# An attention kernel ordered by a planner: other figures for its additions by DMA, a little more lead for the score products, other seeds and one more vector batch

## The chip, the cores and the metric

The kernel runs on one core of one Trainium2 chip. The time is device microseconds of one launch, the median of several runs; one more execution is taken by the hardware profiler, and every profile line here is from such an execution.

## What is computed

Two attention branches over the same 2048 tokens of width 512, with 32 heads of 16, mixed by a gate for each token:

```python
x = A_x
g = sigmoid((x * gate_w).sum(-1, keepdims=True))
# A: softmax attention
scores = einsum("bhqd,bhkd->bhqk", q, k) * 16 ** -0.5
o = einsum("bhqk,bhkd->bhqd", softmax(scores), v)
a = o.reshape(B, S, D) @ A_wo
# B: linear attention, phi(t) = [softmax(t @ w_phi), softmax(-t @ w_phi)]
kv, z = einsum("bhsf,bhsd->bhfd", phi_k, v), einsum("bhsf->bhf", phi_k)
o = einsum("bhqf,bhfd->bhqd", phi_q, kv) / (einsum("bhqf,bhf->bhq", phi_q, z) + 1e-6)
b = o @ B_wo
return g * a + (1 - g) * b
```

Inputs and output are bf16.

## The kernel before

**Tiles.** Branch A has 2048 tiles of scores, 128 keys by 512 queries of one head. Four of them (four heads, on four strips of 32 rows of TensorE) are a pack; 512 packs make 32 groups of 16, and a group's value products gather in one PSUM bank, its accumulator. Most tiles go to ScalarE: TensorE multiplies two (`_qk`, L1185) into a ring of four PSUM banks, ScalarE takes the exponential of both at once into the ring `ET` of 16 slots (`_exp`, L1233), and TensorE multiplies four slots by `V` (`_pv`, L1296). An exponential may write a slot only when the value product that reads it is done.

**Vector batches.** The other tiles go to VectorE in batches of four (`_vector_batch`). For each tile TensorE makes the scores in a bank outside the ring, and VectorE turns them into the bits of an approximate exponential: `v_bits` (L1043) scales and rounds to a 16-bit integer, one tile or two neighbouring banks at a time. The value is a mean over four shifted copies of these bits, so a batch needs three more tiles of integers: `v_step` on VectorE (L1072, four tiles at once), an addition on GpSimd (L1085), or an addition by DMA from the constant `steps` (L1077, 512 KB, issued by GpSimd). Which of them is used goes by the batch's kind. Each of the four copies is multiplied with `V` or `V2` into the group's accumulator (L1296 again, reading `va`, `vb` or the spare memory of `va_wt`, `va_vb`, `vb_on` and `WB`). `NUMS` says how many batches each of the 32 groups has.

**Around them.** Projections (L808, L816, L855, L923) are four products each and an evacuation on VectorE; branch B runs in between (L1457 to L1668, its exponential L1494 on ScalarE); every group ends with a transposition and a division (L1317 to L1349), every four groups with output products (L808 on `WoA` and `WoB`), copies (L1819 to L1829) and stores. Filler products (L1205, L1303) keep TensorE from falling idle.

**The order.** Nothing runs in the order in which it is written. `Plan` holds all operations with a cost, a priority and what they depend on; `order` walks through time, picks on each engine what can start first and, among those, what ranks first, and so writes five queues, one for each engine. Each engine then takes its queue strictly in order, waiting on semaphores. The planner's figures only set the order; on the chip every wait is real. Three of its rules matter here:

- An addition by DMA goes through one channel: it starts `FIRST` after its issue or when the channel is free, takes `MOVES`, and has landed `LANDED` later. What reads its tile is ordered for that time.
- `_late` refuses other work to TensorE if it would end too late for the next score product of ScalarE; `SLIP` moves that border.
- `shift` adds a pseudo-random amount to every priority, from a new entry of `SEEDS` after every 8 packs, so other seeds give another order from the first pack on.

Of the kernel before, what the change touches and what calls it, by code (L numbers as in the profile page):

```python
# [70 lines left out]
class Plan:  # L71
# [6 lines left out]
    SWITCH, PASS, STEP = 0.097, 0.2155, 0.004  # L78
    SPAN, SHARE, FILL = 3.0, 0.58, 0.2155
    PAD, PADS, OVER = 0.45, 2, 0.2  # L80
    SLIP, GAPS, FLOOR = -0.015, 0.65, 0.46

    def __init__(self):
        self.ops = []
# [58 lines left out]
        self.ops.append(o)  # L143
        return o

    SEEDS = (46439, 36297, 2531, 40950, 971, 19659, 43523, 55019, 18035, 35534, 32147, 43513, 5583, 38153, 15135, 20962, 59679, 30439, 26213, 19105, 29455, 34877, 55135, 21414, 3210, 43195, 29993, 1363, 20599, 10691, 26101, 32053, 19915, 10799, 30427, 37694, 56714, 13257, 35679, 20623, 23887, 52907, 36031, 9619, 51019, 11311, 52185, 0, 13385, 43491, 31707, 19759, 44590, 53230, 9789, 22249, 59009, 3577, 57594, 35439, 52351, 16746, 45215, 2875)
    EVERY = 8
    FIRST, LANDED, TURN, HOLD = 1.5, 1.5, 1.9, 30.0

    def shift(self):  # L150

        if len(self.SEEDS) <= self.drawn or self.now < self.EVERY * self.drawn:
            return
        s = self.SEEDS[self.drawn]
        self.drawn += 1
# [329 lines left out]
class _Kernel:  # L485
# [26 lines left out]
    LAST, FIRST_OUT, NEXT_OUT, DEP_OUT = 0, 3, 0, 2  # L512
    ALONE, EARLY = 12, 10
    C_MIX, C_POOL, SPREAD = 15.5, (0.2, 0.0011), 0.9
    C_ADD, MOVES, ADD_AT, PVD, U3 = 0.9, 2.9, -1, 0, 2
    L_MIX, L_BACK, L_PHIT, L_ONTB = 6.5, 0.4, 0.9, 0.4
    TWOS, BEGIN, SPLIT, PSPLIT = 2, 44, 262, 1
    PHIT2, ONTB2, C_PHIT2, C_ONTB2 = 1, 1, 2.3, 1.9
# [460 lines left out]
                prio=100))  # L979
        self.b_gB.writers = done  # L980

    NUMS = (1, 4, 5, 4, 4, 5, 4, 5, 4, 5, 4, 6, 5, 4, 4, 5, 5, 5, 5, 4, 4, 5, 4, 5, 4, 5, 5, 5, 6, 6, 5, 4)

    def _plan_vector(self):

        NT, away = self.NT, []
        for g in range(self.NPACK // NT):
            n = self.NUMS[g]
            rest = self.REND if g == self.NPACK // NT - 1 else self.REST
# [885 lines left out]
```

## Time and profile before

| | |
|---|---|
| median of 3 runs | 724.36 us (723.66 to 725.03) |
| the profiled execution | 723.53 us, of which the span from first to last instruction is 721.7 |
| TensorE / VectorE / ScalarE / GpSimd busy | 694.0 / 691.5 / 706.4 / 447.8 us |
| exponentials of two tiles (L1233, 128x1024) | 730, 674.9 us |
| `v_bits` of one tile / of two | 458 / 63 |
| additions by DMA (L1077) | 157 |
| TensorE's clock | 1.00 throughout |

A row of the page's groups names a line, the engine and the operation, what is written and read (buffer numbers left out), the count, the busy time, the mean of one, and the idle time just before with what ended it. "PE ps L1185" is TensorE, writing PSUM, at line 1185. PEld is TensorE's weight load, which runs beside its products. The chain of waits follows the last instruction back through what released it. Instructions of one engine overlap a little at their ends, so a duration is longer than the pitch at which they follow each other.

### The profile page before, as it was taken

The page shows a single profiled execution, that of the slowest core. Times are in us where ns is not written, and L with a number is a line of the kernel's source. Part 1 is how long each engine was busy: PE and PEld are TensorE (multiplying, and loading weights), DVE is VectorE, ACT ScalarE, POOL GpSimd, SP SyncE. Part 2 cuts the span into 40 slices and gives each one's busy share as a digit, 9 for nine tenths or more (in the row PEclk, how much of TensorE's full clock was granted, in tenths as well). Part 3 has the DMA queues.
Part 4 walks back from the last instruction along what each step waited for, and adds up shares of the span by engine and source line. Part 5 has one row for each costly group of instructions (what it writes and reads, how often), then busy time and mean ns, then how long its engine had stood idle before and what let it go on. Part 6 is the DMA issues. An engine that isn't in the chain of part 4 may idle for free.

```text
span 721.7 us, 17384 instructions
## 1 busy us (share of the span) xinstructions
PE 694.0 (96%) x7312; PEld 211.7 (29%) x7375; DVE 691.5 (96%) x1143; ACT 706.4 (98%) x756; POOL 447.8 (62%) x567
## 2 busy tenths in 40 slices
PE   8999999999999999999999999999999999999998
PEld 3332232222333222222222233232323232223222
DVE  4999999999999999999999999999999999999997
ACT  5999999999999999999999999999999999999996
POOL 3332566665675747485768775768758678477552
PEclk9999999999999999999999999999999999999999
DMA  9623676684966778966768877678678577868873
GB/s 226 155 50 74 123 136 119 116 158 94 189 117 118 147 143 169 187 121 118 140 122 157 166 146 146 105 147 159 114 135 163 112 155 147 151 129 150 165 139 88
DMA packets 68557, 99.17 MB, mean 137 GB/s; under 512 B 42752, under 2 KB 47872, under 8 KB 68480
## 3 DMA queue, kind: packets, MB, share of 16 engines
q0 software_dynamic: 22608, 82.32, 60.4%
q1 hardware_dynamic: 44000, 14.96, 10.3%
q8 instruction: 57, 0.93, 0.5%
q10 hardware_dynamic: 1872, 0.79, 0.5%
q14 instruction: 20, 0.16, 0.1%
HBM read 4.21 MB, written 2.10 MB: 9 GB/s over the span
## 4 chain that ended last, share of the span: by engine, by line
ACT 65%; PE 20%; DVE 7%; DMA 3%; POOL 2%; issue 1%; SPq 1%; POOLq 0%
ACT ET L1233 63%; PE ps L1185 7%; PE ps L1296 7%; PE ps L808 5%; ACT bq L1494 2%; DVE va L1043 2%; DVE vb L1072 1%; DMA va<-steps 1%; DMA vb<-steps 1%; SPq L673 1%; DMA xT<-in_A_x_dram 1%; DVE va_vb L1043 1%; POOL va L1077 0%; DVE onB L1668 0%; PE ps L923 0%
## 5 line engine op out<-in xcount | busy, mean ns | idle before, releaser
L1233 ACT ACTIVATE ET<-ps 128x1024 bf16<-128x1024 f32 (+1 forms) x734 | 677.1, 1084 | 3.1 <-PE ps L1185 1.6
L1043 DVE TENSOR_SCALAR va<-ps 128x512 uint16<-128x512 f32 (+1 forms) x438 | 312.6, 745 | 13.1 <-PE ps L1185 12.1
L1185 PE MATMUL ps<-qT,kT 32*128 32x512 bf16 (+1 forms) x2052 | 292.3, 384 | 13.3 <-ACT ET L1233 7.7
L1077 POOL DMA_DIRECT2D va<-steps x106 | 107.1, 1061 | 103.6 <-DVE vb L1072 50.2
L1185 PEld LDWEIGHTS ps<-qT,kT 32*128 32x128 bf16 x2052 | 74.0, 91 | 277.5 <-ACT ET L1233 255.8
L1296 PE MATMUL ps<-ET,V 128*32 128x512 bf16 x1464 | 141.9, 388 | 0.7 <-DVE va L1043 0.7
L1072 DVE TENSOR_SCALAR vb<-va 128x2048 uint16<-128x2048 uint16 x147 | 100.3, 695 | 0.2 <-PE ps L1296 0.2
L1296 PE MATMUL ps<-va,V 128*32 128x512 bf16 x984 | 92.3, 384 | 0.3 <-DVE vb L1072 0.3
L1296 PE MATMUL ps<-vb,V 128*32 128x512 bf16 x896 | 84.1, 384 | 0.6 <-DMA vb<-steps 0.3
L1085 POOL TENSOR_TENSOR vb<-vb,steps 128x512 int32<-128x512 int32 x50 | 64.0, 1299 | 26.7 <-DVE vb L1072 19.2
L1296 PEld LDWEIGHTS ps<-ET,V 128*32 128x32 bf16 x1464 | 36.4, 94 | 66.9 <-issue 59.0
L808 PE MATMUL ps<-WB,xT 128*128 128x512 bf16 x164 | 49.6, 383 | 3.6 <-issue 2.4
L1498 POOL TENSOR_TENSOR btree<-btree 128x512 f16<-128x512 f16 (+1 forms) x32 | 30.3, 947 | 22.2 <-DVE vb L1072 12.7
L1303 PE MATMUL ps<-kT,zero 128*32 128x512 bf16 x492 | 43.1, 383 | 0.0
L1077 POOL DMA_DIRECT2D vb<-steps x28 | 33.7, 1203 | 8.2 <-PE ps L808 3.7
L808 PE MATMUL ps<-xT,WA 128*128 128x512 bf16 x102 | 32.4, 384 | 2.0 <-issue 1.3
L1043 DVE TENSOR_SCALAR va_vb<-ps 128x512 uint16<-128x512 f32 (+1 forms) x47 | 33.7, 734 | 0.1
L1296 PEld LDWEIGHTS ps<-va,V 128*32 128x32 bf16 x984 | 24.3, 95 | 27.9 <-issue 20.8
L1494 ACT ACTIVATE bq<-bq 128x2048 bf16<-128x2048 bf16 x16 | 31.4, 1960 | 0.0
L899 POOL TENSOR_SCALAR qT<-qT,mask 128x512 bf16<-128x512 bf16 x30 | 22.8, 761 | 12.1 <-DVE qT L895 6.2
L1296 PEld LDWEIGHTS ps<-vb,V 128*32 128x32 bf16 x896 | 22.0, 95 | 24.3 <-issue 14.3
L1043 DVE TENSOR_SCALAR va_wt<-ps 128x512 uint16<-128x512 f32 (+1 forms) x36 | 25.9, 738 | 0.1
(123 smaller groups left out, 721.2 us busy)
## 6 DMA issues: line engine op xcount, KB each, us to landing
va<-steps POOLq DMA_DIRECT2D x106, 512.0 KB, 6.3
vb<-steps POOLq DMA_DIRECT2D x28, 512.0 KB, 7.0
va_wt<-steps POOLq DMA_DIRECT2D x10, 512.0 KB, 5.9
va_vb<-steps POOLq DMA_DIRECT2D x10, 512.0 KB, 5.5
WB<-in_B_wqkv_dram SPq DMA_DIRECT2D x1, 1536.0 KB, 8.2
vb_on<-steps POOLq DMA_DIRECT2D x3, 512.0 KB, 6.7
out_dram<-outt SPq DMA_DIRECT2D x12, 128.0 KB, 6.3
WA<-in_A_wqkv_dram SPq DMA_DIRECT2D x2, 384.0 KB, 4.4
```

The costliest lines, as they stand in the source:

```text
L808: return e.matmul(out, lhs, rhs, start=start, stop=stop)
L899: x = self.plan.op("POOL", lambda e, side=side: e.tensor_scalar(self.qT[:, s0 + side, :], raw, self.mask[:, side:side + 1], 0.0, op0=ALU.m ...
L1043: bits = lambda e, to, src: e.tensor_scalar(to, src, SCALE * LOG2E * 128.0, float(ORIGIN), op0=ALU.mult, op1=ALU.add)
L1072: o = op("DVE", lambda e: e.tensor_scalar(whole(dst), whole(va), float(by), None, op0=ALU.add), 0.16 + n * QCH * 0.00026, reads=reads, wri ...
L1077: o = self.dma("POOL", f"add{number}_{k}", lambda e: e.dma_start(tile[:, 0:n], self.steps[:, 0:n], accum_op=ALU.add), cost=self.C_ADD, rea ...
L1085: o = op("POOL", lambda e, lo=lo, hi=hi: e.tensor_tensor(whole(v3)[:, lo:hi].bitcast(I32), whole(v1)[:, lo:hi].bitcast(I32), whole(self.st ...
L1185: return e.matmul(out[:, cols], self.kT[32 * i:32 * i + 32, cp, kt * TOK:(kt + 1) * TOK], self.qT[32 * i:32 * i + 32, s, cols], start=True ...
L1233: o = plan.op("ACT", lambda e: e.activation(self.ET[:, a % NS:a % NS + n, cols], self.ps[:, a % NR:a % NR + n, cols], ACT.Exp, scale=SCALE ...
L1296: ins = e.matmul(self._bank(ot)[32 * i:32 * i + 32, :], v[:, v0:v0 + 32], tile, start=(kt == 0), stop=(kt == self.NT - 1), tile_position=( ...
L1303: ins = e.matmul(self._bank(ot)[32 * i:32 * i + 32, :], self.zero[:], self.kT[:, 0, 0:QCH], start=False, stop=False, tile_position=(0, 32 ...
L1494: op("ACT", lambda e: e.activation(flat, flat, ACT.Exp), 1.789, reads=[b], writes=[b], name="b_exp", prio=due + 1)
L1498: + [("b_sum", two(128 * n), lambda e, n=n: e.tensor_tensor(half[:, :, 0:n], half[:, :, 0:n], half[:, :, n:2 * n], ALU.add), (n <= self.P_ ...
```

## The change

Four constants and two tables differ; no operation of the kernel is written differently.

```diff
-    SLIP, GAPS, FLOOR = -0.015, 0.65, 0.46
+    SLIP, GAPS, FLOOR = -0.04, 0.65, 0.46
...
-    SEEDS = (46439, 36297, 2531, 40950, 971,
...
+    SEEDS = (20645, 24735, 11770, 21495, 24798,
...
-    FIRST, LANDED, TURN, HOLD = 1.5, 1.5, 1.9, 30.0
+    FIRST, LANDED, TURN, HOLD = 1.4, 1.2, 1.9, 30.0
...
-    C_ADD, MOVES, ADD_AT, PVD, U3 = 0.9, 2.9, -1, 0, 2
+    C_ADD, MOVES, ADD_AT, PVD, U3 = 0.9, 2.85, -1, 0, 2
...
-    NUMS = (1, 4, 5, 4, 4, 5, 4, 5, 4, 5, 4, 6, 5, 4, 4, 5, 5, 5, 5, 4, 4, 5, 4, 5, 4, 5, 5, 5, 6, 6, 5, 4)
+    NUMS = (2, 4, 5, 5, 4, 5, 4, 4, 5, 4, 5, 4, 5, 4, 5, 5, 4, 5, 4, 5, 4, 5, 4, 5, 5, 5, 5, 5, 5, 6, 6, 4)
```

All 64 seeds are others. `NUMS` adds up to 147 where it was 146, so four tiles of scores go from ScalarE to VectorE, and it spreads them otherwise: the first group has two batches for one. Since the seeds and the planner's figures reach every choice, nearly the whole of TensorE's, VectorE's and GpSimd's queues stands in another order. By number of instructions the built program has 728 exponentials of two tiles for 730, 466 `v_bits` of one tile for 458 and 61 of two for 63, 236 `v_step` for 235, 159 additions by DMA for 157, and 118 passes of filler products at L1303 for 123.

The prediction shows TensorE's order at two places, the first 19 us and the end. In its rows L1185 is a product of scores, L1296 a product of values (reading `ET` it is ScalarE's tile, reading `va`, `vb`, `WB` a vector batch's), L808 with `WA` a projection of queries or keys, with `WoA` and `WoB` the output, and L923 a projection of values.

At the start, TensorE before, from the last-but-one score row ahead of the first value product:

```order
L1185 MATMUL ps<-qT,kT 128x512 x3
L923 MATMUL ps<-WA,xT 128x2x128 x4
L1185 MATMUL ps<-qT,kT 128x512 x3
L1296 MATMUL ps<-ET,V 32x512 x8
L923 MATMUL ps<-WA,xT 128x2x128 x8
L808 MATMUL ps<-xT,WA 128x512
L1185 MATMUL ps<-qT,kT 128x512 x3
```

and in the change, from the score row that holds the same two tiles of ScalarE as the third row above:

```order
L1185 MATMUL ps<-qT,kT 128x512 x3
L808 MATMUL ps<-xT,WA 128x512
L923 MATMUL ps<-WA,xT 128x2x128 x8
L1296 MATMUL ps<-ET,V 32x512 x4
L923 MATMUL ps<-WA,xT 128x2x128 x4
L1296 MATMUL ps<-ET,V 32x512 x4
L1296 MATMUL ps<-va_96,V 32x512 x4
L1296 MATMUL ps<-ET,V 32x512 x4
L1185 MATMUL ps<-qT,kT 128x512 x4
```

A projection and eight products of values' projections moved from behind the first value product to ahead of it. At the end, TensorE's rows from the last scores on, before:

```order
L1185 MATMUL ps<-qT,kT 128x512 x2
L808 MATMUL ps<-WoA,onTA 128x512 x3
L808 MATMUL ps<-WoB,WT 128x512 x2
L1296 MATMUL ps<-ET,V 32x512 x4
L1296 MATMUL ps<-va_100,V_67 32x512 x4
L1296 MATMUL ps<-va_97,V_67 32x512 x4
L1296 MATMUL ps<-vb_104,V_67 32x512 x4
L808 MATMUL ps<-WoB,WT 128x512 x2
L808 MATMUL ps<-WoA,onTA 128x512 x6
L808 MATMUL ps<-WoB,WT 128x512 x4
L808 MATMUL ps<-WoA,onTA 128x512 x7
```

and in the change:

```order
L1185 MATMUL ps<-qT,kT 128x512 x2
L1296 MATMUL ps<-ET,V 32x512 x4
L1296 MATMUL ps<-va_96,V_67 32x512 x4
L1296 MATMUL ps<-ET,V 32x512 x4
L1296 MATMUL ps<-WB,V_67 32x512 x4
L1296 MATMUL ps<-ET,V 32x512 x8
L1296 MATMUL ps<-va_97,V_67 32x512 x4
L1296 MATMUL ps<-vb_101,V_67 32x512 x4
L1296 MATMUL ps<-va_98,V_67 32x512 x4
L808 MATMUL ps<-WoB,WT 128x512 x4
L808 MATMUL ps<-WoA,onTA 128x512 x13
```

Before, 5 output products stand between the last scores and the last exponential's value product, and 19 behind the last value product; in the change none and 17, so 7 moved ahead of the last scores.

More of the change, by code (lines that the diff above doesn't have):

```diff
@@ L144, in op @@
         return o
-    SEEDS = (46439, 36297, 2531, 40950, 971, 19659, 43523, 55019, 18035, 35534, 32147, 43513, 5583, 38153, 15135, 20962, 59679, 30439, 26213, 19105, 29455, 34877, 55135, 21414, 3210, 43195, 29993, 1363, 20599, 10691, 26101, 32053, 19915, 10799, 30427, 37694, 56714, 13257, 35679, 20623, 23887, 52907, 36031, 9619, 51019, 11311, 52185, 0, 13385, 43491, 31707, 19759, 44590, 53230, 9789, 22249, 59009, 3577, 57594, 35439, 52351, 16746, 45215, 2875)
+    SEEDS = (20645, 24735, 11770, 21495, 24798, 57639, 39767, 34826, 20859, 44155, 52338, 33183, 53515, 39123, 29127, 37122, 1099, 17207, 36203, 5703, 52058, 34843, 7471, 28503, 58027, 39163, 28279, 57222, 57234, 36322, 36955, 4803, 37407, 40227, 14797, 24150, 35511, 21954, 11343, 9845, 38167, 791, 56855, 27221, 49278, 20251, 58495, 48113, 23517, 41183, 44671, 35093, 13874, 3235, 32949, 53535, 26359, 52383, 21199, 31586, 32878, 1351, 27747, 20999)
     EVERY = 8
-    FIRST, LANDED, TURN, HOLD = 1.5, 1.5, 1.9, 30.0
+    FIRST, LANDED, TURN, HOLD = 1.4, 1.2, 1.9, 30.0
     def shift(self):
```

## The prediction, made before the result was known

> **What bounds the kernel now.** I read the page first: the span, the busy time of each engine, and the rows of 40 slices that say where an engine is not full.
>
> ```profile
> span 721.7 us, 17384 instructions
> PE 694.0 (96%) x7312; PEld 211.7 (29%) x7375; DVE 691.5 (96%) x1143; ACT 706.4 (98%) x756; POOL 447.8 (62%) x567
> DVE  4999999999999999999999999999999999999997
> ACT  5999999999999999999999999999999999999996
> ```
>
> ScalarE is the fullest, and it is short of full only in the first and the last slice. The next view, busy time by stretch, and the groups of ScalarE alone in the same stretch, say how short it is between them:
>
> ```profile
> 19.00:713.00 694.00, 672.22 (x7179) 202.86 (x7241) 677.80 (x1117) 693.56 (x740) 440.45 (x549) 1.00 0.71 136
> L1233 ACT ACTIVATE ET<-ps 128x1024 bf16<-128x1024 f32 x723 | 668.2, 1088 | 0.4
> 200.00:300.00 100.00, 96.88 (x1052) 28.62 (x1055) 99.56 (x166) 100.00 (x109) 65.18 (x81) 1.00 0.78 148
> 500.00:600.00 100.00, 95.73 (x1072) 28.84 (x1072) 98.87 (x163) 99.80 (x106) 71.46 (x91) 1.00 0.74 140
> ```
>
> The columns are the stretch, its length, then the busy time of PE, PEld, DVE, ACT and POOL, the clock, the DMA engines' share and GB/s. From 19 to 713 us ScalarE works 693.56 of 694.00 us: it has lost 0.44 us in the whole middle of the kernel. VectorE has 16.2 us idle there and TensorE 21.8, and from 200 to 300 us VectorE ran 99.56% full while ScalarE lost nothing. So the time is three pieces: the start until ScalarE runs without a gap, the sum of its exponentials, and the tail behind the last of them. What is taken from ScalarE shortens the kernel, provided nothing new makes it wait.
>
> **The change: work taken and given.** The prices are pitches in the chain of waits, where instructions follow without a gap; durations in the groups overlap their neighbours and would count too much.
>
> ```profile
> 147.83 35.78 ACT ET L1233 x39
> 108.16 1.13 DVE va L1043
> 110.09 0.60 DVE vb L1072
> 110.83 1.80 DVE va L1043 x3
> ```
>
> One exponential of two score tiles costs 35.78 / 39 = 0.917 us, a 512-wide `v_bits` 1.80 / 3 = 0.60, a 1024-wide one 1.13, a `v_step` 0.60. The built order has 728 exponentials of two tiles where 730 stood: ScalarE loses 2 x 0.917 = **1.83 us**. VectorE gets 8 more `v_bits` of one tile, 2 fewer of two and one `v_step` more: 8 x 0.60 - 2 x 1.13 + 0.60 = 3.1 us. Those lie in the 16.2 us that it idles beside ScalarE; without that cover they would cost 3.1 us, and that is a rival below. TensorE multiplies the same number of score and value tiles with five filler passes and one whole-array filler fewer, about -1.3 us at the 0.22 us a pass of the tail (below), off the path. GpSimd issues two more additions of 512 KB (159 for 157); they move beside a middle that uses 0.71 of the DMA engines.
>
> **The start moves.** Here the order decides, not the sums. Before:
>
> ```profile
> 12.01 0.39 PE L808 MATMUL ps<-xT,WA 128*128 128x512 bf16 x1 [0.44 <-DMA xT<-in_A_x_dram]
> 16.87 0.39 PE L1185 MATMUL ps<-qT,kT 32*128 32x512 bf16 x3
> 17.19 0.61 PE L1296 MATMUL ps<-ET,V 128*32 128x512 bf16 x8
> 17.74 1.05 PE L923 MATMUL ps<-WA,xT 128*128 128x256 bf16 x8
> 18.62 0.38 PE L808 MATMUL ps<-xT,WA 128*128 128x512 bf16 x1
> 12.76 3.83 ACT L1233 ACTIVATE ET<-ps 128x1024 bf16<-128x1024 f32 x4 [0.39 <-PE ps L1185]
> 17.64 2.85 ACT L1233 ACTIVATE ET<-ps 128x1024 bf16<-128x1024 f32 x3 [1.05 <-PE ps L1296]
> ```
>
> ScalarE waits twice: 0.39 us at 12.76, for scores that TensorE issues behind a projection that waits for `xT`, and 1.05 us at 17.64, for the first value product (L1296), which frees the slot of `ET` that the next exponential writes. In the order of the change, shown above, one projection (L808) and two V projections of four products (L923) stand between the same score row and the first value product, where none stood: 0.22 us and 18.62 - 17.74 = 0.88 us, so it comes 1.10 us later behind that row. The score row itself comes earlier: the projection that waited for `xT` at 12.01 now stands behind later scores, so ScalarE's 0.39 us goes, and with it the row is no longer bound by TensorE's own work at 16.87 but by ScalarE, about 0.5 us earlier. Net 1.10 - 0.5 = **+0.6 us**. The bounds are 1.10 (nothing earlier) and 0.2, what is left if both gains are had in full (the row 0.5, and 0.39 at the wait). Two batches now lie in the first group for one, so VectorE has three more operations ahead of that product, 1.8 us. Its waits there, before, are the cover, 2.7 us in all:
>
> ```profile
> 11.14 1.22 DVE L1043 TENSOR_SCALAR va<-ps 128x1024 uint16<-128x1024 f32 x1 [1.15 <-PE ps L1185]
> 14.52 0.69 DVE L1043 TENSOR_SCALAR va<-ps 128x512 uint16<-128x512 f32 x1 [1.56 <-PE ps L1185]
> ```
>
> **The tail moves.** Before, from the last value products on:
>
> ```profile
> 708.45 4.95 ACT L1233 ACTIVATE ET<-ps 128x1024 bf16<-128x1024 f32 x5
> 713.45 0.40 PE L1296 MATMUL ps<-ET,V 128*32 128x512 bf16 x4
> 714.50 4.22 PE ps L808 x19
> 718.74 0.60 ACT L1819 ACTIVATE xT<-ps 128x512 bf16<-128x512 f32 x1 [0.48 <-PE ps L808]
> ```
>
> The last exponential ends at 713.40, four value passes follow, then 19 output products at 4.22 / 19 = 0.22 us, then the last copy. In the change's order, shown above, four value passes (the second half of `ET` x8, `va_97`, `vb_101`, `va_98`) still follow the last exponential, but 17 output products for 19: 2 x 0.22 = 0.44 us less. The four closing products now come together, so two copies of 0.60 us queue on ScalarE; I give back 0.1 and take **-0.35 us**. It could be 0: `vb_101` is the last addition that GpSimd issues, and if it lands late, the tail waits for it.
>
> **The waits for landings.** The planner counts an addition alone on the channel as landed `FIRST` + `MOVES` + `LANDED` after its issue: 1.5 + 2.9 + 1.5 = 5.9 us before, 1.4 + 2.85 + 1.2 = 5.45 now. These rows tell, of the additions' line, how long the issue takes for one group of them (shortest, median and longest, in ns), how long they take to land and who waited, and then one such wait:
>
> ```profile
> L1077 POOL DMA_DIRECT2D vb<-steps x28: 852/1164/2230, 69.9 to 686.5; - x28
> DMA to landing us min/median/max: 4.5/6.4/13.1
> PEld ps L1296: 2.9, 9
> PE ps L1296: 0.3, 1
> 501.45 0.40 PE L1296 MATMUL ps<-vb,V 128*32 128x512 bf16 x4 [0.31 <-DMA vb<-steps]
> 500.96 7.43 ACT L1233 ACTIVATE ET<-ps 128x1024 bf16<-128x1024 f32 x8
> ```
>
> Ten of 157 landings were waited for, 3.2 us in all, and the one that left TensorE's products idle, at 501.45, left no gap on ScalarE (the last row is eight exponentials without one). With figures 0.45 us shorter, a product stands that much earlier in TensorE's order, and TensorE takes its queue in order: score products behind a late tile wait, and ScalarE for them. 4.5 us is still well under 5.45; the late ones are those that share the channel. If the ten waits become 30 of about 0.45 us, 13.5 us of TensorE's 21.8 idle us go to them. ScalarE feels only what exceeds TensorE's lead, which `SLIP` raises by 0.025 us. The bounds are 0 (as now) and 4 us (a third of the 13.5 gets through); nearest to the rows above, where nothing got through, I take **+0.2**.
>
> Sum: -1.83 + 0.6 - 0.35 + 0.2 = -1.4 us. The profiled execution took 723.53 us, 1.8 over its span, so it would be 722.1; it is 0.8 under the median of the runs shown, and from the median 724.36 - 1.4 = **722.9 us**.
>
> **Rivals.** *The landings get through* (slower). The mechanism is the last paragraph's: thirty tiles multiplied before they have landed. It decides the sign once TensorE waits for additions more than about 10 us in all; at 13.5 with a third passed on, the term is 4 and the time 726.7. For it: the median landing, 6.4, lies above the figure for a lone addition, so most share the channel, and 13.1 is far above it. Against it: nothing passed on at 3.2 us. The Trainium skill, SBUF — State Buffer, section SBUF: two separate sides, says that VectorE in a two-port mode keeps GpSimd from writing a DMA's descriptors until it ends. By that, a fuller VectorE makes issues longer and landings later; the trace shows issues of `vb` between 0.85 and 2.23 us, which agrees but does not show the cause.
>
> *VectorE becomes the bound* (slower). If its 16.2 idle us cannot shrink, because they are waits for scores, its 3.1 us lengthen the middle instead of ScalarE's 1.83 shortening it: 724.36 + 3.1 + 0.6 - 0.35 = 727.7. For it: 677.80 + 3.1 of 692.2 us is 98.4%. Against it: the 99.56% from 200 to 300 us.
>
> *The gain is eaten* (no change). The start costs its upper bound, 1.10, the tail gains nothing, the landings cost 0.5: -1.83 + 1.1 + 0.5 = -0.2, 724.1. For it: the start's order is plain, and so small a gain needs every other term right.
>
> *More than forecast.* The lead removes the middle's 0.44, the start costs 0.2, no landing is felt: -1.83 + 0.2 - 0.35 - 0.4 = -2.4, 722.0.
>
> **How the numbers follow.** A measurement of this kernel tells about 0.2% (1.45 us) from no change, so 722.9 lies on the edge of it. The forecast, with what lies up to 0.7 us around it, has 0.38; more than forecast 0.20; the gain eaten 0.14; the landings 0.18; VectorE 0.10. Faster is two thirds of the first and all of the second, 0.45; no change the rest of the first and the third, 0.27; slower the last two, 0.28. The likeliest case alone is 722.3 to 723.6. The range, 721.7 to 726.7, reaches to the first rival's price and leaves out VectorE's and the best of the fourth.
>
> **What would show it.** In the profile of the changed kernel: 728 exponentials of two tiles; a single wait of ScalarE of about 2 us near 18 us that ends on L1296, and none for scores at 12.8; from there to the last exponential ScalarE within 1 us of full; fewer than 25 waits of TensorE for additions; 17 output products at the end of the chain. The forecast is wrong if ScalarE's idle time between 19 us and its last exponential exceeds 2 us, or if the start's wait is 3 us.

## The result, and the profile after

The changed kernel took 728.62 us (median of 5, 726.78 to 729.07) against 724.01 us of the kernel before, run beside it: ratio 1.0057, 95% interval 1.0041 to 1.0074. It is **slower by 0.57%**. The prediction was 722.9 us with a range to 726.7. The profiled execution took 726.78 us, so it is the quickest of the five, and its span is 724.9.

The first page of the changed kernel: span, busy times, two rows of slices, and the chain that ended last by engine; behind it that chain of the kernel before.

```profile
span 724.9 us, 17362 instructions
PE 693.3 (96%) x7299; PEld 213.0 (29%) x7366; DVE 693.8 (96%) x1150; ACT 704.9 (97%) x754; POOL 448.6 (62%) x569
DVE  5999999999999999999999989999999999999996
ACT  5999999999999999999999999999999999999996
DVE 36%; ACT 26%; PE 24%; DMA 8%; POOL 4%; issue 1%; POOLq 0%
```

```profile
ACT 65%; PE 20%; DVE 7%; DMA 3%; POOL 2%; issue 1%; SPq 1%; POOLq 0%
```

Busy times and slices look as before; the chain doesn't. ScalarE made up 65% of it and now makes up 26%, and transfers (DMA) went from 3 to 8%. ScalarE alone from 19 to 716 us, two stretches, and what TensorE waited for on the additions' line:

```profile
L1233 ACT ACTIVATE ET<-ps 128x1024 bf16<-128x1024 f32 x722 | 667.9, 1094 | 6.3 <-PE ps L1185 3.5 <-PE ps L1296 2.2
200.00:300.00 100.00, 95.64 (x978) 28.57 (x986) 97.00 (x163) 98.84 (x106) 66.49 (x89) 1.00 0.72 135
500.00:600.00 100.00, 96.40 (x1070) 29.10 (x1079) 99.24 (x169) 99.80 (x107) 72.41 (x89) 1.00 0.77 145
PEld ps L1296: 9.4, 20
PE ps L1296: 3.6, 8
DMA to landing us min/median/max: 4.5/6.3/14.0
```

ScalarE idles 6.3 us where it idled 0.4. 2.2 of them are the start, the rest lies in the middle (100.00 busy from 200 to 300 us before, 98.84 now). TensorE's waits for additions went from 3.2 us in 10 waits to 13.0 in 28, while the transfers land much as before (4.5/6.4/13.1 then). This sum is a measure and not a loss: where weight load and product both stand still, both rows count it, and a weight load often stands 0.23 us without any landing. The products alone (PE) waited 0.3 us in 1 wait before and 3.6 in 8 now. VectorE's load alone does not do it: from 500 to 600 us it is 99.24% full and ScalarE still 99.80.

One stall, TensorE first and then ScalarE:

```profile
266.24 0.39 PE L1185 MATMUL ps<-qT,kT 32*128 32x512 bf16 x2
266.55 0.40 PE L1296 MATMUL ps<-ET,V 128*32 128x512 bf16 x4
267.87 0.40 PE L1296 MATMUL ps<-va,V 128*32 128x512 bf16 x4 [0.92 <-DMA va<-steps]
268.20 0.39 PE L1185 MATMUL ps<-qT,kT 32*128 32x512 bf16 x3
```

```profile
254.63 13.11 ACT L1233 ACTIVATE ET<-ps 128x1024 bf16<-128x1024 f32 x14
268.63 1.94 ACT L1233 ACTIVATE ET<-ps 128x1024 bf16<-128x1024 f32 x2 [0.89 <-PE ps L1185]
```

A value product waits 0.92 us for its tile, the next scores stand behind it in TensorE's queue, and ScalarE pays 0.89 of it.

Idle time isn't all: exponentials overlap their neighbours, so one can start late by 0.1 us without an idle row. The table therefore sums, over all neighbouring exponentials from 19 us on, what their pitch exceeds the usual 0.904 us. Below it is the account of the two spans (3.2 us apart).

| us, from the profiled executions | before | after |
|---|---|---|
| the exponential that ends the start's wait | 17.64 | 18.44 |
| pitch above 0.904, summed | 11.98 | 16.08 |
| last exponential's end to the span's end | 8.34 | 8.32 |

Two exponentials fewer are 2 x 0.904 = -1.8, the start is +0.8, the pitch +4.1, the tail 0: together +3.1.

### The profile page after: what moved, and what is told of

Read it like the earlier page. It is cut to its first block, busy times and chain, and to the rows that moved or that the text cites. A ratio compares the mean times of both kernels' runs of the same rounds, so it can differ in the third digit from the quotient of the medians.

```text
span 724.9 us, 17362 instructions
## 1 busy us (share of the span) xinstructions
PE 693.3 (96%) x7299; PEld 213.0 (29%) x7366; DVE 693.8 (96%) x1150; ACT 704.9 (97%) x754; POOL 448.6 (62%) x569
## 4 chain that ended last, share of the span: by engine, by line
DVE 36%; ACT 26%; PE 24%; DMA 8%; POOL 4%; issue 1%; POOLq 0%
ACT ET L1233 25%; DVE va L1043 16%; PE ps L1296 9%; PE ps L1185 8%; DMA va<-steps 6%; DVE vb L1072 5%; PE ps L808 4%; DVE va_vb L1043 2%; DVE va_wt L1043 1%; ACT bq L1494 1%; DMA vb<-steps 1%; DVE WB L1072 1%; DVE bq L1457 1%; DVE kT L882 1%; DVE T L1317 1%
## 5 line engine op out<-in xcount | busy, mean ns | idle before, releaser
L1185 PE MATMUL ps<-qT,kT 32*128 32x512 bf16 (+1 forms) x2052 | 289.9, 385 | 10.2 <-ACT ET L1233 7.3
L1185 PEld LDWEIGHTS ps<-qT,kT 32*128 32x128 bf16 x2052 | 73.5, 91 | 273.7 <-ACT ET L1233 248.6
L1296 PE MATMUL ps<-ET,V 128*32 128x512 bf16 x1460 | 142.0, 388 | 1.6 <-DVE T L1317 0.3
L1296 PE MATMUL ps<-va,V 128*32 128x512 bf16 x992 | 93.3, 384 | 3.7 <-DMA va<-steps 3.2
L1296 PE MATMUL ps<-vb,V 128*32 128x512 bf16 x904 | 85.0, 383 | 1.6 <-DVE vb L1072 0.7
L1085 POOL TENSOR_TENSOR vb<-vb,steps 128x512 int32<-128x512 int32 x50 | 67.8, 1379 | 17.8 <-DVE vb L1072 10.4
L1296 PEld LDWEIGHTS ps<-ET,V 128*32 128x32 bf16 x1460 | 36.9, 94 | 68.2 <-issue 58.3
L808 PE MATMUL ps<-WB,xT 128*128 128x512 bf16 x163 | 50.5, 384 | 3.5 <-issue 2.1
L1498 POOL TENSOR_TENSOR btree<-btree 128x512 f16<-128x512 f16 (+1 forms) x32 | 37.3, 1165 | 14.1 <-DVE btree L1496 12.3
L1303 PE MATMUL ps<-kT,zero 128*32 128x512 bf16 x472 | 42.1, 384 | 0.0
L1043 DVE TENSOR_SCALAR va_vb<-ps 128x512 uint16<-128x512 f32 (+1 forms) x43 | 31.3, 743 | 3.3 <-PE ps L1185 3.1
L1296 PEld LDWEIGHTS ps<-va,V 128*32 128x32 bf16 x992 | 25.0, 95 | 31.9 <-issue 15.1
L808 PE MATMUL ps<-xT,WA 128*128 128x512 bf16 x101 | 31.9, 383 | 2.5 <-issue 1.7
L1296 PEld LDWEIGHTS ps<-vb,V 128*32 128x32 bf16 x904 | 22.8, 96 | 25.0 <-issue 12.6
L1043 DVE TENSOR_SCALAR va_wt<-ps 128x512 uint16<-128x512 f32 (+1 forms) x37 | 28.5, 779 | 0.7 <-PE ps L1185 0.7
```

The costliest lines, as they stand in the source:

```text
L808: return e.matmul(out, lhs, rhs, start=start, stop=stop)
L1043: bits = lambda e, to, src: e.tensor_scalar(to, src, SCALE * LOG2E * 128.0, float(ORIGIN), op0=ALU.mult, op1=ALU.add)
L1085: o = op("POOL", lambda e, lo=lo, hi=hi: e.tensor_tensor(whole(v3)[:, lo:hi].bitcast(I32), whole(v1)[:, lo:hi].bitcast(I32), whole(self.st ...
L1185: return e.matmul(out[:, cols], self.kT[32 * i:32 * i + 32, cp, kt * TOK:(kt + 1) * TOK], self.qT[32 * i:32 * i + 32, s, cols], start=True ...
L1296: ins = e.matmul(self._bank(ot)[32 * i:32 * i + 32, :], v[:, v0:v0 + 32], tile, start=(kt == 0), stop=(kt == self.NT - 1), tile_position=( ...
L1303: ins = e.matmul(self._bank(ot)[32 * i:32 * i + 32, :], self.zero[:], self.kT[:, 0, 0:QCH], start=False, stop=False, tile_position=(0, 32 ...
```

## Experiments

Theory: the landings, as in the prediction's first rival. Rivals: the other order and VectorE's load; the luck of the drawn order. "Waits" are TensorE's waits for additions, the two rows above added up. Ratios are to the kernel before, run beside each. Code is cut to the lines that matter; text in brackets or plain words stands for code.

**Half of each addition, order untouched.** The same edit was made in both kernels; it leaves the second half of those tiles' shifted copies out of the result.

```diff
-e.dma_start(tile[:, 0:n], self.steps[:, 0:n], accum_op=ALU.add)
+e.dma_start(tile[:, 0:n // 2], self.steps[:, 0:n // 2], accum_op=ALU.add)
```

> The changed kernel with its order untouched; each addition by DMA adds only the first half of its columns (256 KB for 512 KB), so the second half of those tiles' shifted copies is left out of the computation. Theory 'landings' (TensorE meets value products of tiles that have not landed, and ScalarE's scores stand behind them in its queue): the landings come about 1 us earlier, TensorE's waits for additions (13 us in the changed kernel) fall below 5 us, ScalarE's idle time between 19 us and its last exponential falls from 4.1 to under 1.6 us, and the time falls by 2.3 to 3.2 us against the changed kernel's 728.6, to 725.4 to 726.3. Rival 'VectorE and order' (the extra batch and the new places of VectorE's work make the gaps): ScalarE's idle time there stays above 3.4 us and the time stays within 0.7 us of 728.6.

> Control: the kernel before with its order untouched and the same half of each addition by DMA left out. Both theories: ScalarE lost only 0.4 us in the middle, so at most 0.4 us can come back; time within 0.7 us of the kernel before. If it is faster by over 1.5 us, then half additions help in some other way than by landing in time, and the run of the changed kernel with half additions says less than it seems.

Changed kernel with half additions: 724.25 us, ratio 0.9999 (0.9990 to 1.0007), so 4.4 us came back, more than the 2.3 to 3.2 expected. Kernel before with half additions: 724.20, ratio 1.0001 (0.9992 to 1.0011), nothing. The changed kernel's view of the additions' line and ScalarE's group:

```profile
PEld ps L1296: 0.2, 1
DMA to landing us min/median/max: 3.3/3.7/6.9
L1233 ACT ACTIVATE ET<-ps 128x1024 bf16<-128x1024 f32 x722 | 667.5, 1101 | 4.1 <-PE ps L1296 2.2 <-PE ps L1185 1.3
```

The waits are gone (0.2 us), and with them the whole difference in time. Since the other kernel gains nothing, less traffic as such is worth nothing. ScalarE's idle time in the middle is 1.9 us for 4.1, above the 1.6 expected: not all gaps were landings.

**Three quarters.**

> The changed kernel with its order untouched; each addition by DMA adds only the first three quarters of its columns (384 KB), so the last quarter of those tiles' shifted copies is left out. A dose between the whole additions (landing 6.3 us in the middle, 728.6 us) and the half ones (3.7 us, 724.25 us). Theory 'landings': landing about 5.0 us in the middle, TensorE's waits for additions 2 to 6 us, time 724.8 to 726.6, that is over half of the 4.4 us back for half of the bytes taken, since the waits are a tail of a distribution and its worst go first. A rival, traffic: the time is linear in the bytes, 726.4.

725.09 us, ratio 1.0012 (1.0003 to 1.0021); waits 1.9 us in 3, landing 3.9/4.8/10.8. A quarter of the bytes gives back 3.5 of the 4.4 us, which is no line in the bytes: the first quarter is worth most. The pitch above 0.904 sums to 13.91 us here and 13.25 with halves.

**The start alone.**

```diff
+q = p.queues["PE"]; at = next(k for k, o in enumerate(q) if o.name == "pv0"); q.insert(at - 1, q.pop(at))
```

> The changed kernel, computing everything: in TensorE's queue the first value product is moved ahead of the projection of values (four products) that stood directly ahead of it. If ScalarE's single wait at the start (2.23 us at 18.4 us) is set by what stands ahead of that value product, it falls by the 0.44 us that four such products take, to about 1.8 us, and the time by 0.3 to 0.5 us, which is at the edge of what the timing tells; the wait itself is read from the profile. If the wait is set by the tile of the exponential or by VectorE, it stays at 2.2 us.

728.94 us, ratio 1.0065 (1.0051 to 1.0080): the timing shows none of the 0.3 to 0.5 us expected. The wait before the exponential after the first value product fell from 2.23 to 1.79 us, as expected, so that product's place sets it.

**Products moved later.** The first try moved each value product of an added tile behind the next score product, wherever that stood:

```diff
+for o in (the value products of tiles with an addition by DMA):
+    end = place of the next "qk" in TensorE's queue, or of the last operation before one that depends on o
+    q.insert(end, q.pop(q.index(o)))
```

> The changed kernel, computing everything: only in TensorE's queue, each value product of a tile that was added to by DMA is moved behind the next product of ScalarE's scores, wherever nothing in between depends on it. Theory 'landings': about 0.9 us more slack for each landing, so waits of TensorE for additions fall from 13 us to under 6, ScalarE's idle time in the middle falls from 4.1 to under 2 us, time down by 1.8 to 3 us, to 725.6 to 726.8. Rival 'VectorE and order': no change over 0.7 us, since VectorE's and GpSimd's queues and ScalarE's work are the same; a third possibility is slower, if the moved products now hold back the slots and banks that VectorE writes next.

770.13 us, ratio 1.0639 (1.0621 to 1.0657): 42 us slower, though the waits fell to 2.5 us in 7. TensorE became the bound. Its group of scores from 19 to 713 us, changed kernel first, this one behind it, and this one's chain:

```profile
L1185 PE MATMUL ps<-qT,kT 32*128 32x512 bf16 x2014 | 284.8, 385 | 9.8 <-ACT ET L1233 7.3 <-DVE va L1043 0.5 <-DVE btree L1480 0.4
```

```profile
L1185 PE MATMUL ps<-qT,kT 32*128 32x512 bf16 x1880 | 309.4, 386 | 9.3 <-ACT ET L1233 4.2 <-DVE va L1043 1.0 <-issue 0.8
PE 70%; ACT 16%; DVE 9%; DMA 3%; issue 2%; POOL 1%; POOLq 0%
```

Fewer products (the window is the same, the run longer) take longer: score products that follow each other run side by side, and a stretch of them takes 0.32 us whether it has two or three (266.24 to 266.55 above; 268.20 to the next row, 268.52). The edit cut stretches in two, 840 of them in the trace for 723; 117 more at 0.32 us are 37 of the 42. Moved behind whole stretches instead, where nothing in between depends on the product, once for all tiles with an addition and once for the 25 late ones. Late is a tile whose weight load began within 0.07 us of its landing in the first profile.

```diff
-    end = place of the next "qk" in TensorE's queue
+    end = end of the next stretch of score products
```

> The changed kernel, computing everything. In TensorE's queue the value products of the 25 tiles that were waited for in the profile of the changed kernel each move behind the next whole row of score products (the earlier run had split those rows; here none is split), where nothing in between depends on them. Theory 'landings': the time comes down towards what the half additions gave, 724.3: I expect TensorE to wait for additions under 5 us in all (13 in the changed kernel), ScalarE's idle time from 19 us on under 2.8 us of 4.0 behind the start's wait, and 725.0 to 726.8 us. Rival 'half as many bytes helped in another way than by landing in time' (less traffic beside the engines): no change over 0.7 us from 728.6.

> As the run with the picked tiles, but the value products of all tiles that were added to by DMA move behind the next whole row of score products. If splitting rows was what made the earlier run of this kind 45 us slower (159 products by about 0.29 us of TensorE), this one, which splits none, stays within 3 us of the changed kernel. Theory 'landings': TensorE's waits for additions under 4 us, time 725 to 727.5; a loss against the picked ones would come from VectorE, which gets banks and tiles back one row later (0.5 to 1 us for each such tile). If instead moving value products later is itself the cost, whatever it splits, it is slower by tens of us again.

25 tiles: 729.56 us, ratio 1.0073 (1.0060 to 1.0086), waits 9.7 us in 20, where 725.0 to 726.8 us and under 5 were expected. All tiles: 732.47, ratio 1.0127 (1.0109 to 1.0145), waits 8.6 in 16, slower than its expectation too. Splitting was what cost 42 us; but later products are no gain. With the 25, the gap at 268.6 is gone, and others have come. One of them in TensorE's rows:

```profile
73.57 0.39 PE L1185 MATMUL ps<-qT,kT 32*128 32x512 bf16 x3
74.73 0.40 PE L1296 MATMUL ps<-vb,V 128*32 128x512 bf16 x4 [0.77 <-DMA vb<-steps]
```

That tile is none of the 25. Its addition had landed 6.28 us after its issue in the first profile and took 7.45 here. What made it later here was not looked into.

**Additions issued earlier.**

```diff
+for o in (the additions in GpSimd's queue):
+    move o ahead of up to 3 vector operations, if the planner has its tile ready before them
```

> The changed kernel, computing everything, with the queues of TensorE, VectorE, ScalarE and SyncE untouched. In GpSimd's queue each addition by DMA moves ahead of up to three vector operations of GpSimd that stand directly ahead of it, where by the planner's own times its tile was ready before they began. In the profile of the changed kernel 15 of the 25 tiles that were waited for had their addition issued without any idle time of GpSimd ahead of it, so behind such an operation, 0.3 to 1.3 us each. Theory 'landings': the additions that can move land about 1 us earlier, TensorE's waits for additions fall from 13 us to 5 to 9, the time from 728.6 to 725.5 to 727.5. Rival 'what GpSimd does is late next' (operations behind the additions, each 0.9 us later, hold up branch B, qT or the normalization): no change or slower, with new waits of TensorE or VectorE for GpSimd's operations.

743.35 us, ratio 1.0269 (1.0255 to 1.0283). Waits for additions by DMA fell to 5.8 us in 11, as expected, but the rival came true. Two rows of this kernel's waits and one of its timeline:

```profile
PEld ps L1296 <- POOL vb L1085: 5.2, 6, 1.8
PEld ps L1296 <- POOL WB L1085: 3.9, 4, 1.5
188.56 0.62 PE L1296 MATMUL ps<-vb,V 128*32 128x512 bf16 x4 [1.46 <-POOL vb L1085]
```

GpSimd's own additions (L1085) stood behind the issues, and TensorE waited for those instead.

**The figures apart from the draw.** The three figures exchanged in both kernels (the diff shows the kernel before), a pair without seeds, and `SLIP` alone in it:

```diff
-FIRST, LANDED = 1.5, 1.5 ; MOVES = 2.9
+FIRST, LANDED = 1.4, 1.2 ; MOVES = 2.85
```

> The changed kernel with the three figures for additions as before (1.5, 1.5, 2.9), all else (SLIP, seeds, batches) as changed; the planner writes another order. Theory 'the figures put the products too near': TensorE's waits for additions fall from 13 us to under 8 us, whatever the new order costs elsewhere. Rival 'luck of the order': they stay at 10 to 16 us. The time itself says little, since these seeds were not drawn for these figures: 725 to 735 us.

> The kernel before with the three figures for additions as changed (1.4, 1.2, 2.85), all else as before; the planner writes another order. Theory 'the figures': TensorE's waits for additions rise from 3.2 us to over 8 us. Rival 'luck of the order': they stay under 6 us. The time: 725 to 735 us, and little is read from it alone.

> The kernel before without seeds (priorities as written), the figures for additions as before (1.5, 1.5, 2.9). One half of a pair that differs in the three figures alone. An order without drawn seeds is slow, 760 to 800 us by the two runs with figures and seeds exchanged; what is read is TensorE's waits for additions: I expect 5 to 11 us.

> The other half of the pair: without seeds, figures as changed (1.4, 1.2, 2.85), all else as the kernel before. Theory 'the figures': at least 4 us more of TensorE's waits for additions than its pair, as with the seeds of before (3.2 to 15.7 us) and the reverse of the seeds of the change (13.0 to 10.7). Rival 'luck of the order': the difference is within 2 us or of the other sign.

> The kernel before without seeds, figures for additions as before, SLIP alone as changed (-0.04 for -0.015). Against the run without seeds and with the old figures, where TensorE waited 4.1 us, 8 times, for additions: if the lead of the score products has no part in it, 2 to 6.5 us; if it has, nearer to the 10.1 us, 22 times, that the new figures gave. The time says little, 775 to 800 us.

| seeds | waits, old figures | waits, new figures | time, old and new |
|---|---|---|---|
| of before | 3.2 us, 10 | 15.7, 33 | 724.0 and 792.0 |
| of the change | 10.7, 14 | 13.0, 28 | 774.9 and 728.6 |
| none | 4.1, 8 | 10.1, 22 | 780.7 and 794.3 |

All three pairs go the same way and the number of waits at least doubles, so the figures raise them; the size depends on the draw. With the change's seeds it is 2.3 us, and the 10.7 us left there lie where luck of the order was expected to leave them (10 to 16), not under 8: for these seeds most of the sum stays with the old figures. `SLIP` alone gave 5.7 us in 12 waits, inside the expectation for no part in it. The new spread of `NUMS` was not tried alone. The times of exchanged orders lie 50 to 70 us above the kernel before (without seeds from one execution each) and have other stalls (one exponential waits 16.9 us for a value product): a table of seeds is only good for the figures with which it was drawn.

**Three stalls undone, and the changed kernel again.**

```diff
+p.later({52}); p.sooner(3, {131})      # one value product, one addition
+q.insert(at - 1, q.pop(at))            # the first value product, as above
```

> The changed kernel, computing everything, with three single edits of the written order: the value product that TensorE waited 0.92 us for at 267.9 us moves behind the next row of score products; the addition whose product TensorE waited 0.96 us for at 607.7 us is issued ahead of two small vector operations of GpSimd (0.69 us together) that stood ahead of it; the first value product moves ahead of four projection products, as in the earlier run. Theory 'landings', read stall by stall: ScalarE's gaps of 0.89 us at 268.6 and 0.95 us at 608.5 shrink to under 0.1 and 0.5, the start's wait from 2.2 to 1.8 us; 1.7 to 2.3 us less than the changed kernel in the same call, 726.3 to 727.2. Rival 'stalls are only shifted': the gaps go there, but others of the same sum come behind them, and the time stays within 0.7 us of the changed kernel's.

> The changed kernel itself once more, for a second profile and as the base of this call. If landings scatter from one execution to the next, its time is 728 to 729.5 us with a wider scatter than the kernel before or the half additions, ScalarE's gaps between 19 us and the last exponential sum to 4 to 6 us, and the tiles that are waited for are partly others than in the first profile. If the stalls are a fixed property of the order, the same tiles are late by the same times within 0.1 us.

Undone: 727.01 us, ratio 1.0044 (1.0028 to 1.0061). Again: 728.23, ratio 1.0048 (1.0035 to 1.0062), waits 13.8 us in 27. ScalarE's rows with the stalls undone:

```profile
259.64 14.96 ACT L1233 ACTIVATE ET<-ps 128x1024 bf16<-128x1024 f32 x16
593.96 17.55 ACT L1233 ACTIVATE ET<-ps 128x1024 bf16<-128x1024 f32 x19
```

The gaps at 268.6 and 608.5 are gone. The time is 1.2 us lower than the unchanged kernel's beside it, between the two theories (1.7 or more, under 0.7), and the intervals overlap: the profile shows the single prices, the timing doesn't settle them. In the second profile of the unchanged kernel 21 of the 25 tiles are late again, and only 6 of 159 additions land over 0.5 us earlier or later. So the late tiles are a property of the program.

**Code loads.** What makes them late stands in the page of the changed kernel and in its transfers from 255 to 272 us (queue, packets, MB, share of the DMA engines):

```profile
q8 instruction: 57, 0.93, 0.5%
```

```profile
q0 software_dynamic: 416, 1.51, 47.2%
q8 instruction: 1, 0.02, 0.4%
```

57 times, 16 KB of instructions are loaded, on average once for about 256 of TensorE's, each for 0.96 us (median) as one packet, so on one DMA engine. The addition whose tile stalled TensorE at 267.87 was issued at 261.14 with no other on the channel, and landed 6.69 us later; a load ran from 265.82 to 266.80. Fifteen of the addition's sixteen last packets had ended by 265.36, the sixteenth ended at 266.81, with the load. Where the value product was moved (the run of the three stalls), the load began as the last packets ended, and the addition took 5.20. Over all 159, 40 have a load that ends between their first packet and their last; they land 1.1 us (median) later than 4.55 us after the issue or 2.5 us after the landing before, whichever is later; the others 0.1; 19 of the 25 late tiles are among the 40. To test it, the loads were moved against an unchanged order (the 14 waits become 7 instructions in the trace behind each product, 63 in all; the other two runs have 28 for 14, so 126):

```diff
-    ins = e.matmul(... self.warm ...)
+    ins = e.matmul(... self.warm ...); [e.wait_ge(*w) for w in self.plan.again for _ in range(14 * (n > 3))]
```

> The changed kernel, computing everything, all five queues in the same order; among TensorE's nine filler products of the first 5 us stand 63 instructions more (waits on a value that is reached already), so each later load of TensorE's instructions comes 63 instructions earlier, about 3 us. Theory 'code loads': which additions land late moves with the loads. Of the 25 tiles waited for in the first profile, 9 to 14 land over 0.5 us earlier after their issue, while over 20 others land over 0.5 us later; the waits of TensorE for additions go to other tiles and are 12 to 18 us in all, the time 728 to 731 us. Rival 'order and channel alone': each addition lands within 0.5 us of its time in the first profile save for fewer than 12, as between the two profiles of the unchanged kernel (8 of 159 by over 0.4 us), and the time stays within 0.7 us of 728.4.

> The same with 126 instructions more, so the loads stand about half a period of 12.7 us away. Theory 'code loads': of the 25 tiles 11 to 16 land over 0.5 us earlier, over 30 others over 0.5 us later; TensorE's waits 14 to 20 us in all, the time 729 to 732 us, if the order was one whose loads happened to fall well. Rival as above.

> The kernel before with 126 such instructions more. Theory 'code loads': its additions move too (over 40 of 157 land over 0.5 us earlier or later), but its value products stand 0.45 us and more further behind their issue, so TensorE's waits for additions stay under 6 us (3.2 in the first profile) and the time within 1 us of the kernel before: the longer figures were the room for the loads. If the time rises by 2 us or more, the old figures gave no such room either, and only the drawn order did.

| | 63 more | 126 more | unchanged, again |
|---|---|---|---|
| of the 25 late tiles, land over 0.5 us earlier | 13 | 17 | 1 |
| additions that land over 0.5 us later | 34 | 52 | 3 |
| of the 25, late again | 9 | 3 | 21 |
| waits, us | 10.5 in 24 | 16.8 in 35 | 13.8 in 27 |

With 63 instructions more the loads come a median of 33.5 of TensorE's weight loads earlier, with 126 more 65; a product is one weight load and one matmul, so that is the whole shift, and the loads are TensorE's. In both runs 38 additions have a load that ends between their packets, only 4 and 2 of the 25 among them, and again these land 1.05 us late (median) and the rest 0.1. The late tiles follow the loads, so the loads cause most of them. In the kernel before, 39 additions meet a load and land 1.0 us late too, with waits of 3.2 us; with 126 more 101 of 157 landings move by over 0.5 us, yet the waits are 4.3 us in 7. The waits of the run with 63 (12 to 18 expected) and all three times were expected wrongly, the times because the added waits delay the first exponentials: 732.48 us (ratio 1.0121), 739.85 (1.0220) and 736.40 (1.0170), of which 4.75, 11.61 and 11.29 are the later start in the profiles (the exponential after the first value product). Without it they would be 727.7, 728.2 and 725.1: each kernel within 1.1 us of itself.

## Why the prediction was wrong

**Bound and work** held: ScalarE sets the time, and two exponentials fewer take 1.8 us off.

**The start** was the right mechanism, +0.8 for +0.6, within its bounds; a wait of 2.23 us on L1296 as forecast. In TensorE's and ScalarE's rows:

```profile
16.48 0.39 PE L1185 MATMUL ps<-qT,kT 32*128 32x512 bf16 x3
16.80 0.39 PE L808 MATMUL ps<-xT,WA 128*128 128x512 bf16 x1
17.02 1.04 PE L923 MATMUL ps<-WA,xT 128*128 128x256 bf16 x8
17.99 0.40 PE L1296 MATMUL ps<-ET,V 128*32 128x512 bf16 x4
```

```profile
18.44 2.85 ACT L1233 ACTIVATE ET<-ps 128x1024 bf16<-128x1024 f32 x3 [2.23 <-PE ps L1296]
```

The kernel before's rows are in the prediction. From score row to first value product it is 1.51 us for 0.32, so 1.19 later (1.10 forecast), and the row stands 0.39 earlier (0.5).

**The tail** gave 0 for -0.35. Its two products fewer hide nothing:

```profile
717.75 0.72 DVE L1317 STREAM_TRANSPOSE T<-ps 128x512 f32<-128x512 f32 x1 [2.76 <-PE ps L1296]
719.46 0.71 DVE L1349 STREAM_TRANSPOSE onTA<-T 128x512 bf16<-128x512 bf16 x1
720.86 1.34 DVE L1823 TENSOR_TENSOR xT<-ps,xT 128x512 bf16<-128x512 f32 x2 [0.69 <-PE ps L808]
721.08 1.09 ACT L1819 ACTIVATE xT<-ps 128x512 bf16<-128x512 f32 x2 [4.48 <-PE ps L808]
```

The closing products need `onTA`, ready at 720.17, and it follows the last value product through VectorE's five steps, not through the output products beside them. In the kernel before these steps took as long:

```profile
714.55 0.72 DVE L1317 STREAM_TRANSPOSE T<-ps 128x512 f32<-128x512 f32 x1 [1.04 <-PE ps L1296]
716.26 0.71 DVE L1349 STREAM_TRANSPOSE onTA<-T 128x512 bf16<-128x512 bf16 x1
```

`onTA` was ready at 716.97, and in both kernels the span ends 4.7 us behind it. This is read from the traces; no run tested it.

**The landings are the step that failed.** The text foresaw 30 waits of 13.5 us in all; there were 28 of 13.0, with the double counting said above, so TensorE's products did not idle 13.5 us but 3.6. It then took +0.2 us for what ScalarE feels, "nearest to the rows above, where nothing got through". The half additions put it at 4.4 us in the medians, at 16.08 - 13.25 = 2.8 in the first profile, which is the quickest of its five, and at 17.33 - 13.25 = 4.1 in the second (728.23 us): near the rival's price of 4. The row it leaned on was one wait of 0.31 us that left no gap on ScalarE. Of the new ones 0.25, 0.92 and 0.96 us passed on as 0.25, 0.89 and 0.95, and 0.49 as 0.35; four of 0.19 to 0.33 us left no gap. So most of what the products idled got through. A share of the whole sum was the wrong form, and that the rival's third of it came near was luck: each wait of a product has to be set against the lead at its place.

The other misreading is "4.5 us is still well under 5.45; the late ones are those that share the channel". A lone addition met by a code load takes 4.5 + 1.1 = 5.6 us, which lies between the old figure, 5.9, and the new one. The kernel before has the same loads and keeps its waits small, so the room that the change took away is room for the loads. How much of the 4.4 us is the figures and how much the drawn order stays open: the exchange of the figures changes the whole order, and with the change's seeds 10.7 us of waits stay with the old ones.

**VectorE's cover** did not hold quite: with next to no landing waited for, the pitch is still 1.3 us above that of the kernel before (13.25 for 11.98; 11.65 with its own half additions). The prediction had nothing for this. The largest rest of it, in TensorE's and VectorE's rows of the changed kernel:

```profile
356.06 1.00 PE L1296 MATMUL ps<-vb,V 128*32 128x512 bf16 x12 [0.69 <-DVE vb L1072]
354.69 0.69 DVE L1541 TENSOR_TENSOR bq<-bq,brec 128x1024 bf16<-128x1024 bf16 x1 [0.93 <-POOL brec L1529]
```

VectorE waited 0.93 us for GpSimd and was late with `vb`, and ScalarE lost 0.68 us at 357.42, as it did with half additions (0.67). That speaks for the order and not the load, but no run tested it; the rival's 3.1 us did not come. What the runs leave: -1.8, +0.8, 0, +1.3 and 4.0 to 4.4 for the landings (728.23 or 728.62 less 724.25), together +4.3 to +4.7 for the 4.6 measured. The prediction's own sign of being wrong came: ScalarE idled 4.1 us in the middle, over the 2 that it named. Of the rivals, the landings' was right in mechanism and in the size of its term; it was given 0.18.

No version beat both kernels. Even with half additions, where no landing is waited for to speak of, the change is only level with the kernel before.

## What to carry to other kernels

A planner's figure for a transfer is not the time of a lone transfer: what it holds above that is room for whatever else uses the DMA engines, and it should be cut by what the late landings measure, not by the minimum or the median. Where an engine takes its queue in order, price a wait by the lead at its place; a wait that was harmless in one row says nothing of the next. Before moving products apart, count what each separate stretch costs.

## What was unexpected of the hardware

Loads of TensorE's own instructions delay transfers of data by 1.0 to 1.2 us (median) where one ends among a transfer's packets, 35 to 40 times in the runs counted (the two kernels, the second run of the changed one and the three with added waits), and where they meet moves with the number of TensorE's instructions.

An addition by DMA of 256, 384 and 512 KB lands after 3.25, 3.89 and 4.51 us at the least: 2.0 us and 0.63 for each 128 KB, 208,000 bytes a microsecond. The Trainium skill, DMA: Bandwidth & Descriptors, section Anatomy of one DMA — SWDGE (gpsimd) path, gives 2.0 us and 436,000 bytes a microsecond for a transfer. The fixed part agrees with these runs; their rate is half of it.

A wait that is already met is not free on TensorE: the added ones mostly follow each other at 0.106 us in the traces. 63 of them moved the first exponential from 7.58 to 12.28 us and 126 to 19.08; part of that is the products behind them, which ran at half the rate there (0.43 us apart for 0.21).
